# Another order of the same instructions in a fused adaLN block: V of the first pair loaded ahead of a LayerNorm group's transposes

## The chip, the cores and the metric

The kernel runs on one core of one Trainium2 chip. The metric is device time in microseconds, lower is better. Engines named below: PE (TensorE, matmuls and transposes), DVE (VectorE), ACT (ScalarE), POOL (GpSimd) and SP (SyncE, which here only issues DMAs). L851 is line 851 of the kernel.

## What is computed

One block on x of 2048 rows and 512 columns, in bf16, with six modulation vectors (sa, ca, ga, sb, cb, gb) made from one conditioning vector c:

```python
mod = (silu(c) @ w_mod).reshape(1, 6, 1, 512)          # sa, ca, ga, sb, cb, gb
h = layernorm(x) * (1 + ca) + sa
x = x + ga * A(h)      # 32 heads of 16, each row attends to itself and 7 rows before it, two apart
h = layernorm(x) * (1 + cb) + sb
x = x + gb * B(h)      # (silu(h @ w1) * (h @ w3)) @ w2, 1792 inner columns
```

In A, `qkv = h @ wqkv`; logits are `q . k / 4` over the 8 rows `s, s-2, ..., s-14` (rows before the first are masked), softmax over these 8, a weighted sum of v, and a product with `wo`.

## The kernel before

**Tiling.** The 2048 rows are 16 tiles of 128. Tile T holds the rows of one residue class modulo 16, so that a step of two rows is a step of one tile: tiles 0 to 7 are the even class, tiles 8 to 15 the odd one, and a tile's attention needs tiles of its own class only. SBUF holds all weights; `kT` holds k transposed for all rows.

**First stage, per group of tiles (`LN1`, L269: tiles 0-1, 2-3, 4-7, 8-11, 12-15).** `ln_stats` (L549) takes mean and variance on DVE (L555, L556), the power on POOL (L563, L565) and the normalised tile on DVE (L570). `ln_T` (L603) turns these into h: the first three groups by transposes on PE (L630) and a pass that applies the modulation on the way out of PSUM (DVE L645 or ACT L638); tiles 8-11 and 12-15 by four DMA transposes each (SP, L612 by the helper's L124) and four ACT passes (L615) that need all four. `proj_qk` (L669) makes q and k (PE L685, ACT copies L694 and L695), `proj_v` (L699) makes v (PE L705, ACT copy L715) and stores it to a scratch in DRAM. Four tiles share one q buffer: a product that reads it waits for the copies of all four.

**Attention, per pair of tiles (`BLOCKS`, L266).** `logits` (L727): DVE multiplies q with eight shifted k's (L742, L744), about 2.3 us a tile, and PE adds up within heads (L753). `shift`, `exps` and `softmax` (L760 to L814): maximum, difference, exponential on ACT (L783), sum, reciprocal and product on DVE, a turn on PE (L808) and a copy on ACT (L812). `values` (L816): two DMAs of 512 KB each load V of a tile from the scratch, already shifted (L823); they need the stores of all eight V tiles of the class and a free buffer of three. DVE multiplies with the weights (L829, called AV below, 2.29 us a tile), PE adds up (L839), ACT copies (L845), a DMA transposes (the tile `sb_ot`), PE multiplies with `wo`, scaled by ga before (L941, L851), and DVE adds to x with the row sum (L855).

**FFN, per group (`FFN`, L265: tiles 0-1, 2-3, 4-7, 8-11, 12-13, 14-15).** `ln_sums` (L576) on POOL and ACT (L580 to L595), `ln_T` again: by PE for the first two groups, by DMA transposes and ACT L615 for the others. `ffn_unit` (L860) makes one of 14 column groups: PE L867 for w1 and for w3, ACT silu (L873), DVE product (L876). `ffn_w2` (L883) multiplies with w2 (PE L908, at the end L896), and the result is scaled, added to x and stored.

**What sets the order.** `_build` lists 1121 operations, numbered as they are listed. `ORDER` (L975) is a permutation of these numbers written out by hand: `place` (L143) goes through it and appends each operation to its engine's queue, and `SLOTS` (L1024) gives each value its PSUM bank (0 to 7) or its buffer. Engines run their queues in this order; an operation waits for what it reads and for the last users of the bank or buffer that it takes over. So the order of each queue decides which wait stands in front of what. `GATES` (L974) adds dependencies to four weight loads. All DMAs but one are issued from SP's queue.

```python
for i in order: ...   # place: self.order[o.eng].append(o)
if before is not None:
    o.prev.extend(before.users)     # wait for the last users of this bank or buffer
```

Of the numbers that the next sections speak of: 368, 369 and 376, 377 are the V loads of tiles 0 and 1; 129, 135, 177, 183, 230, 233, 236, 239 the stores of V tiles 0 to 7; 256 to 259 the DMA transposes of tiles 8 to 11 and 308 to 311 those of tiles 12 to 15; 32 to 35 are loads of `wo`, 37 and 38 of a half each of a part of `w_mod`; 40 to 51 are FFN weights; 356, 358, 384, 386 the products of tiles 0, 1, 2 and 3; 370 and 378 the AVs of tiles 0 and 1; 763 to 766 the DMA transposes of FFN tiles 4 to 7; 513 and 521 the DMA transposes of the attention outputs of tiles 10 and 11; 480, 481, 488, 489, 508, 509, 516, 517 the V loads of tiles 8 to 11.

Of the kernel before, what the change touches and what calls it, by code (L numbers as in the profile page):

```python
# [271 lines left out]
def _build(p, A_x, A_wqkv, A_wo, B_w1, B_w3, B_w2, c, w_mod, out):  # L272
# [801 lines left out]
```

## Time and profile before

| what | value |
|---|---|
| median of 3 runs | 241.52 us (241.07 to 241.82) |
| the profiled execution's own time | 241.19 us |
| its span, first to last instruction | 239.4 us |
| PE busy | 231.6 us, 97% |
| DVE busy | 181.2 us, 76% |
| ACT busy | 142.5 us, 60% |
| POOL busy | 21.7 us, 9% |
| granted clock of PE | 1.00 |

The profile is of one execution. A row of a timeline gives the start, the time drawn, engine, line, operation, what it writes and reads, how many instructions are merged, and in brackets the idle time of the engine before it and what ended it. SPq is the issue of a DMA on SP; the landing is told apart from it (rows that begin with a time and DMA). The table by stage gives each engine's busy time within a stretch.

### The profile page before, as it was taken

What the parts mean: (1) busy time and instruction counts of PE and PEld (TensorE: products, weight loads), DVE (VectorE), ACT (ScalarE), POOL (GpSimd) and SP (SyncE); (2) the same over time, 40 slices, a digit from 0 to 9 for tenths busy, and PEclk for the clock granted to TensorE, in tenths of its full rate; (3) what the DMA queues carried; (4) which work ended last, traced back from release to release, by engine and by line L of the source; (5) the groups of instructions that cost most, each with busy time, mean ns of one, the idle gap of its engine ahead of it and who ended that gap; (6) DMA issues with size and microseconds to landing.
All of it is one profiled execution on the core that took longest, in us unless ns stands there. A gap on an engine that the chain in (4) does not pass through costs nothing.

```text
span 239.4 us, 4562 instructions
## 1 busy us (share of the span) xinstructions
PE 231.6 (97%) x1805; PEld 136.4 (57%) x1805; DVE 181.2 (76%) x309; ACT 142.5 (60%) x277; POOL 21.7 (9%) x63
## 2 busy tenths in 40 slices
PE   7999999899999999998998999999999999999995
PEld 4766454454678766553444445434448447576874
DVE  5689799897999999998969999746528365524562
ACT  2179978759999705975937786453665225451400
POOL 4134100001001000220003101000200002000000
PEclk9999999999999999999999999999999999999999
DMA  6999999969999898585370393613161100200012
GB/s 208 374 328 236 140 252 303 337 195 348 310 249 332 265 276 203 181 218 52 75 232 3 71 329 84 197 31 90 35 170 49 25 22 22 68 0 23 25 60 71
DMA packets 53997, 38.85 MB, mean 162 GB/s; under 512 B 21192, under 2 KB 52952, under 8 KB 53976
## 3 DMA queue, kind: packets, MB, share of 16 engines
q1 hardware_dynamic: 53968, 38.56, 58.1%
q8 instruction: 14, 0.23, 0.4%
q14 instruction: 7, 0.06, 0.1%
q10 hardware_dynamic: 8, 0.00, 0.0%
HBM read 29.62 MB, written 4.21 MB: 141 GB/s over the span
## 4 chain that ended last, share of the span: by engine, by line
PE 60%; DVE 14%; DMA 12%; ACT 6%; SPq 4%; issue 2%; POOL 1%; DVEq 0%
PE pall L867 34%; PE pall L908 14%; DMA sb_vsh<-v_scratch_dram 8%; DVE sb_vsh L829 5%; PE pall L851 4%; SPq L124 4%; DMA sb_wqkv<-in_A_wqkv_dram 3%; DVE sb_st L555 3%; PE pall L839 3%; PE pall L896 3%; DVE sb_pq L744 2%; DMA sb_h<-sb_xn 2%; DVE sb_xn L570 1%; ACT sb_h L615 1%; ACT sb_xn L595 1%
## 5 line engine op out<-in xcount | busy, mean ns | idle before, releaser
L867 PE MATMUL pall<-sb_h,sb_w 128*128 128x256 bf16 (+1 forms) x672 | 102.1, 308 | 1.2 <-ACT sb_h L615 1.2
L867 PEld LDWEIGHTS pall<-sb_h,sb_w 128*128 128x128 bf16 x672 | 64.8, 98 | 36.0 <-ACT sb_h L615 1.6
L876 DVE TENSOR_TENSOR sb_hh<-sb_sg,pall 128x256 bf16<-128x256 bf16 (+1 forms) x84 | 39.4, 504 | 30.8 <-PE pall L867 25.9
L873 ACT ACTIVATE sb_sg<-pall 128x256 bf16<-128x256 f32 (+1 forms) x84 | 35.0, 454 | 37.5 <-PE pall L867 32.4
L908 PE MATMUL pall<-sb_w,sb_hh 128*128 128x512 bf16 x168 | 37.7, 379 | 0.0
L685 PE MATMUL pall<-sb_h,sb_wqkv 128*128 128x512 bf16 (+1 forms) x160 | 31.8, 336 | 0.3 <-DMA sb_wqkv<-in_A_wqkv_dram 0.3
L829 DVE TENSOR_TENSOR sb_vsh<-sb_vsh,sb_al 128x4096 bf16<-128x4096 bf16 x12 | 27.2, 2290 | 5.6 <-DMA sb_vsh<-v_scratch_dram 5.6
L908 PEld LDWEIGHTS pall<-sb_w,sb_hh 128*128 128x128 bf16 x168 | 16.4, 98 | 18.7
L615 ACT ACTIVATE sb_h<-sb_h,sb_modc 128x512 bf16<-128x512 bf16 (+1 forms) x24 | 16.3, 733 | 12.1 <-DMA sb_h<-sb_xn 12.1
L685 PEld LDWEIGHTS pall<-sb_h,sb_wqkv 128*128 128x128 bf16 x160 | 14.9, 98 | 12.3 <-DVE sb_st L555 0.5
L742 DVE TENSOR_TENSOR sb_pq<-sb_q,sb_kT 128x1024 bf16<-128x1024 bf16 (+7 forms) x16 | 21.6, 1352 | 0.2 <-issue 0.2
L744 DVE TENSOR_TENSOR sb_pq<-sb_q,sb_kT 128x3048 bf16<-128x3048 bf16 (+6 forms) x14 | 17.2, 1226 | 0.0
L705 PE MATMUL pall<-sb_wqkv,sb_h 128*128 128x512 bf16 x64 | 16.8, 379 | 0.3 <-ACT sb_h L615 0.3
L584 ACT ACTIVATE sb_xn<-sb_x,sb_nm 128x512 bf16<-128x512 bf16 x16 | 11.4, 715 | 8.9 <-POOL sb_nm L580 8.9
L851 PE MATMUL pall<-sb_wo,sb_ot 128*128 128x512 bf16 x64 | 15.8, 380 | 0.3 <-DMA sb_ot<-sb_ac 0.3
L580 POOL TENSOR_SCALAR sb_nm<-sb_sx 128x2 f32<-128x2 f32 x8 | 1.7, 218 | 141.3 <-DVE sb_x L855 141.3
L595 ACT ACTIVATE sb_xn<-sb_x,sb_nb,sb_rs 128x512 bf16<-128x512 bf16 x16 | 12.6, 806 | 1.6 <-POOL sb_nb L593 1.6
L638 ACT ACTIVATE sb_h<-pall,sb_modc 128x256 bf16<-128x256 bf16 (+1 forms) x16 | 9.0, 625 | 7.0 <-DVE sb_modc L509 5.5
L855 DVE SCALAR_TENSOR_TENSOR sb_x<-pall,sb_x 128x512 bf16<-128x512 f32 x16 | 10.8, 686 | 1.3 <-PE pall L851 1.0
L694 ACT ACTIVATE sb_q<-pall 128x512 bf16<-128x512 f32 x16 | 9.2, 595 | 4.2 <-PE pall L685 4.2
L845 ACT ACTIVATE sb_ac<-pall 128x512 bf16<-128x512 f32 x16 | 9.4, 605 | 3.3 <-PE pall L839 3.3
L851 PEld LDWEIGHTS pall<-sb_wo,sb_ot 128*128 128x128 bf16 x64 | 6.0, 98 | 7.8 <-DMA sb_ot<-sb_ac 0.8
(88 smaller groups left out, 233.3 us busy)
## 6 DMA issues: line engine op xcount, KB each, us to landing
sb_vsh<-v_scratch_dram SPq DMA_DIRECT2D x24, 512.0 KB, 5.2
sb_vshx<-v_scratch_dram SPq DMA_DIRECT2D x8, 512.0 KB, 4.3
sb_w<-in_B_w_dram SPq DMA_DIRECT2D x6, 512.0 KB, 8.1
sb_w<-in_B_w_dram SPq DMA_DIRECT2D x6, 384.0 KB, 4.7
v_scratch_dram<-sb_v SPq DMA_DIRECT2D x16, 128.0 KB, 4.7
out_dram<-sb_o SPq DMA_DIRECT2D x14, 128.0 KB, 1.7
sb_wqkv<-in_A_wqkv_dram SPq DMA_DIRECT2D x6, 256.0 KB, 6.5
sb_x<-in_A_x_dram SPq DMA_DIRECT2D x4, 256.0 KB, 6.6
```

Of the source, the lines that this page charges most:

```text
L595: p.op("act", lambda e, vn=vn, T=T: e.activation(vn.at[:], x_sb[:, T, :], ACT.Identity, bias=nb[:, T, :], scale=rs[:, NT + T, :]), c_act(5 ...
L615: return e.activation(vh.at[:, ft, 0:n * P], vh.at[:, ft, 0:n * P], ACT.Identity, bias=modc[:, 8 * which + ft:8 * which + ft + 1], scale=m ...
L685: ins = e.matmul(bank(vp)[:, j * n:(j + 1) * n], wqkv[:, t, col:col + P], vh.at[:, t, 0:n], start=(t == ORDER[0] and j == 0), stop=(t == O ...
L705: ins = e.matmul(bank(vp), vh.at[:, t, tt * P:(tt + 1) * P], wqkv[:, t, 2 * D:3 * D], start=(t == ORDER[0]), stop=(t == ORDER[-1]))
L742: ins = e.tensor_tensor(o(0, u + 1, 0), q(u + 1, 0), k(T, u + 1, 0), ALU.mult)
L744: ins = e.tensor_tensor(o(u + 1, n, 1), q(n, 1), k(top, n, 1), ALU.mult)
L829: return e.tensor_tensor(v_w, v_w, a_w, ALU.mult)
L851: ins = e.matmul(bank(vy), vt.at[:, ft, :], wo[:, ft, :], start=(ft == 0), stop=(ft == KT - 1))
L867: ins = e.matmul(bank(vp)[:, 0:n], wt[:, t, fi * P:(fi + 1) * P], vh.at[:, t, 0:n], start=(t == 0), stop=(t == KT - 1))
L873: p.op("act", lambda e: e.activation(vt.at[:, 0:n], bank(vgp)[:, 0:n], ACT.Silu), c_act(n), k, r=[vgp], w=[vt], table="silu")
L876: p.op("dve", lambda e: e.tensor_tensor(vh_.at[:, 0:n], vt.at[:, 0:n], bank(vup)[:, 0:n], ALU.mult), c_dve(n), k, r=[vt, vup], w=[vh_])
L908: ins = e.matmul(bank(vz), vhh[fi].at[:, tt * P:(tt + 1) * P], scaled(fi, 0, D) if T >= NT - 4 else w2[:, fi, :], start=(fi == 0), stop=(f ...
```

## The change

`ORDER` and `SLOTS` are replaced; nothing else. Every operation is there once, as before. POOL's queue is the same. The other queues are the same up to the 16th DMA on SP, the 39th operation on PE, the 33rd on DVE and the 5th on ACT, and differ in most places behind that.

SP's queue behind the store of zeros (36), where the two begin to differ, by what each DMA moves:

| before | after |
|---|---|
| wo, wo, wo; V store 0, 3; w_mod gate (39); wo; V store 1 | w_mod half (37); V store 1, 0; wo, wo; w_mod gate (39) |
| transposes 8-11 (four); V store 5, 2 | transpose; V store 2; transpose; V store 6, 3; two transposes |
| two transposes of 12-15; w_mod half (37); V store 6, 4, 7 | V store 5, 4, 7; wo, wo; w_mod half (38) |
| FFN weight (45); two transposes of 12-15 | **V loads 0, 0, 1, 1** |
| **V loads 1, 1, 0**; V store 10; **V load 0** | FFN weights (40, 44); transposes of 12-15 (four) |
| FFN weight (42); w_mod half (38); V store 11, 13 | outputs' transposes of tiles 0, 1; V store 8, 9 |

Later on SP, around the DMA transposes of FFN tiles 4 to 7 (763 to 766) and of the outputs of tiles 10 and 11 (513, 521):

| before | after |
|---|---|
| 763; V loads 517 (tile 11), 481 (tile 8); 764, 765, 766 | V loads 509, 517, 516; 763, 764; V load 508 (tile 10); 765, 766 |
| 513; V load 489 (tile 9); 521; V loads 480, 488 | V load 489; 513; V load 488; 521; V loads 481, 542 (tile 12), 480 |

On DVE the products of tiles 0 and 1 come ahead of three normalised tiles (13, 14, 15) instead of one before and two behind; then follow the softmax, the products of tile 3, the AVs of tiles 0 and 1 and the products of tile 2 (before: products of 3, softmax, products of 2, AV 1, AV 0). On ACT the copy of q that the first products wait for (156) moves from the 18th place to the 27th, behind the copies of k. On PE v of tile 6 is the first of tiles 4 to 7 and v of tile 7 the eighth; `wo` of tiles 0 and 1 stands ahead of all q, k and v of tiles 12 to 15, which begin with q (318).

```diff
 ORDER = [
...
-    91, 92, 93, 94, 96, 100, 80, 95, 81, 82, 97, 101, 83, 98, 99, 84, 86, 85, 87, 119, 114, 104, 136, 138, 102, 109, 103, 36,
-    33, 32, 35, 110, 115, 120, 105, 137, 106, 121, 111, 116, 117, 112, 107, 108, 118, 113, 130, 139, 140, 141, 143, 145, 142,
-    144, 149, 148, 151, 150, 124, 125, 146, 131, 122, 123, 172, 126, 157, 147, 132, 152, 127, 128, 133, 129, 134, 173, 178,
-    179, 180, 158, 181, 167, 162, 163, 182, 183, 39, 34, 135, 184, 186, 185, 187, 194, 192, 195, 193, 188, 189, 191, 201, 207,
-    174, 168, 242, 190, 200, 196, 197, 206, 198, 208, 202, 199, 209, 211, 210, 203, 204, 205, 164, 175, 169, 170, 153, 154,
-    155, 344, 159, 156, 160, 165, 161, 166, 240, 241, 243, 248, 244, 250, 245, 247, 257, 345, 346, 249, 246, 251, 252, 256,
-    292, 294, 253, 255, 254, 259, 258, 295, 293, 296, 300, 297, 226, 227, 231, 232, 233, 171, 176, 177, 222, 223, 302, 301,
-    303, 304, 305, 307, 306, 310, 311, 220, 221, 224, 225, 358, 356, 299, 298, 37, 234, 235, 236, 347, 263, 261, 228, 229,
-    230, 237, 238, 212, 239, 260, 262, 218, 216, 219, 217, 359, 357, 386, 360, 361, 352, 214, 215, 348, 270, 271, 268, 269,
-    362, 363, 286, 287, 264, 276, 353, 354, 45, 309, 308, 314, 313, 277, 312, 364, 289, 365, 366, 367, 213, 377, 376, 369,
-    288, 368, 42, 278, 272, 315, 280, 279, 281, 290, 38, 291, 335, 336, 337, 322, 320, 384, 378, 323, 321, 379, 380, 370, 387,
...
-    755, 757, 764, 652, 503, 504, 717, 725, 756, 698, 718, 758, 505, 759, 730, 726, 760, 658, 731, 732, 761, 765, 506, 733,
-    507, 762, 766, 767, 768, 769, 770, 468, 734, 741, 735, 736, 737, 742, 743, 653, 510, 511, 469, 471, 518, 519, 520, 512,
-    472, 473, 524, 526, 771, 779, 775, 780, 659, 781, 782, 474, 475, 476, 477, 787, 789, 788, 790, 513, 514, 795, 515, 489,
-    521, 480, 803, 522, 523, 478, 479, 482, 488, 490, 799, 800, 823, 825, 791, 792, 824, 793, 796, 801, 525, 491, 527, 859,
...
+    91, 92, 93, 94, 96, 100, 80, 95, 81, 82, 97, 101, 83, 98, 99, 84, 86, 85, 87, 119, 114, 104, 136, 138, 102, 109, 103, 137,
+    110, 105, 115, 120, 121, 106, 116, 111, 122, 123, 124, 139, 140, 141, 143, 145, 142, 144, 146, 149, 148, 150, 147, 117,
+    107, 108, 118, 151, 130, 131, 178, 179, 172, 125, 173, 174, 162, 126, 36, 127, 37, 175, 128, 176, 132, 133, 134, 167, 168,
+    135, 129, 112, 157, 35, 34, 169, 39, 184, 186, 185, 187, 188, 189, 192, 194, 193, 195, 190, 206, 196, 200, 197, 170, 152,
+    191, 207, 201, 199, 203, 209, 198, 113, 171, 208, 211, 240, 241, 242, 243, 250, 248, 244, 245, 247, 257, 177, 202, 205,
+    210, 204, 251, 249, 292, 252, 253, 294, 255, 259, 300, 295, 293, 254, 296, 246, 153, 154, 155, 158, 163, 164, 297, 298,
+    180, 159, 160, 181, 165, 161, 344, 302, 234, 166, 235, 236, 182, 183, 256, 258, 224, 225, 345, 301, 226, 220, 303, 222,
+    304, 227, 305, 221, 223, 156, 358, 356, 231, 232, 233, 228, 229, 230, 237, 238, 239, 306, 307, 299, 261, 263, 262, 260,
+    346, 347, 216, 212, 359, 218, 357, 360, 361, 362, 219, 32, 33, 348, 352, 214, 215, 217, 283, 284, 280, 363, 274, 278, 281,
+    279, 275, 353, 364, 354, 365, 276, 366, 367, 266, 267, 264, 277, 270, 271, 265, 268, 269, 213, 38, 386, 387, 368, 369,
+    370, 371, 372, 377, 286, 376, 378, 379, 287, 380, 40, 44, 308, 311, 310, 309, 312, 315, 313, 355, 314, 349, 272, 273, 384,
...
+    705, 706, 733, 732, 734, 722, 709, 711, 689, 690, 757, 756, 758, 713, 712, 714, 759, 710, 506, 507, 760, 715, 716, 717,
+    761, 653, 765, 762, 766, 769, 768, 767, 770, 735, 718, 736, 737, 741, 742, 468, 518, 510, 471, 519, 469, 472, 473, 511,
+    512, 520, 526, 474, 475, 738, 739, 476, 477, 524, 819, 779, 787, 791, 788, 780, 820, 803, 775, 777, 478, 489, 513, 793,
+    514, 515, 776, 778, 792, 479, 488, 490, 521, 743, 804, 821, 805, 522, 523, 822, 806, 795, 799, 481, 542, 480, 482, 771,
...
 ]
 SLOTS = [
...
-    7, 0, 1, 2, 3, 4, 5, 6, 0, 1, 2, 3, 4, 5, 6, 0, 7, 1, 2, 3, 4, 5, 6, 0, 7, 3, 4, 5, 6, 0, 1, 1, 0, 2, 3, 0, 4, 7, 0, 2, 0,
-    1, 1, 3, 2, 5, 1, 6, 5, 7, 0, 6, 3, 2, 4, 2, 0, 4, 1, 2, 2, 2, 1, 3, 1, 1, 7, 5, 7, 5, 0, 4, 2, 0, 2, 0, 4, 1, 6, 2, 4, 3,
...
+    7, 0, 1, 2, 3, 4, 5, 6, 0, 1, 2, 3, 4, 5, 6, 0, 7, 1, 2, 3, 4, 5, 6, 0, 7, 3, 4, 5, 6, 0, 1, 1, 0, 2, 3, 0, 4, 7, 0, 1, 0,
+    2, 2, 3, 2, 5, 1, 6, 2, 6, 3, 7, 5, 1, 0, 0, 4, 0, 2, 1, 5, 2, 1, 4, 1, 0, 6, 2, 6, 3, 1, 5, 0, 2, 7, 1, 7, 2, 1, 0, 1, 3,
...
 ]
```

96 rows, old and new, of tables (ORDER, SLOTS) are left out of this document.

## The prediction

> **What bounds the kernel now.** I read the table of busy time by stage first, cut where the kind of work changes, then the timeline of PE for what ended each idle stretch, then DVE and the DMA issues (SPq) around each of them.
>
> ```profile
> 10.00:66.00 56.00, 54.94 (x497) 30.82 (x499) 49.96 (x82) 45.48 (x84) 7.72 (x18) 1.00 1.01 275
> 66.00:112.00 46.00, 46.00 (x444) 31.19 (x432) 44.61 (x75) 31.05 (x67) 4.17 (x12) 1.00 0.88 231
> 112.00:132.00 20.00, 17.93 (x130) 8.01 (x123) 17.62 (x20) 14.46 (x26) 2.59 (x4) 1.00 0.34 95
> 132.00:239.43 107.43, 104.81 (x679) 60.77 (x677) 62.62 (x113) 48.86 (x99) 4.51 (x13) 1.00 0.26 76
> ```
>
> The columns behind the length are PE, PE's weight loads, DVE, ACT and POOL, then clock, DMA share and GB/s. PE is idle 1.06 us from 10 to 66, nothing from 66 to 112, 2.07 from 112 to 132; the 2.62 behind 132 lie after its last matmul. The clock is 1.00 throughout. So PE sets the end, and an order of the same instructions can win only what PE waits.
>
> ```profile
> 41.80 1.04 PE L705 MATMUL pall<-sb_wqkv,sb_h 128*128 128x512 bf16 x4 [0.27 <-ACT sb_h L615]
> 46.65 0.61 PE L839 MATMUL pall<-sb_vsh,sb_ind 128*32 128x512 bf16 x8 [0.67 <-DVE sb_vsh L829]
> 113.44 0.82 PE L867 MATMUL pall<-sb_h,sb_w 128*128 128x512 bf16 x3 [1.15 <-ACT sb_h L615]
> 121.66 1.04 PE L851 MATMUL pall<-sb_wo,sb_ot 128*128 128x512 bf16 x4 [0.28 <-DMA sb_ot<-sb_ac]
> 122.76 5.34 PE L867 MATMUL pall<-sb_h,sb_w 128*128 128x512 bf16 x24
> 129.28 0.61 PE L839 MATMUL pall<-sb_vsh,sb_ind 128*32 128x512 bf16 x8 [0.63 <-DVE sb_vsh L829]
> ```
>
> A wait costs more than the idle shown. In the row of 24 matmuls, 5.34 us less one drawn length of 0.38 over 23 steps is 0.216 a matmul, so each drawn end lies 0.16 late. With 0.16 added: 0.43 and 0.83 in the opening, 1.31, 0.44 and 0.79 from 113 to 129: **3.8 us** in five waits, and some 0.3 in one small one at 61.6. That 4.1 is the most that can go.
>
> **The change.** Nothing is added or removed; POOL's order is the same. Everything up to 10 us is the same. Three places matter.
>
> **A, the opening (10 to 66).** The V loads of the first pair move on SP.
>
> ```profile
> 12.35 1.99 SPq L124 DMA_DIRECT2D sb_wo<-in_A_wo_dram  x3
> ...
> 30.42 1.49 SPq L124 DMA_DIRECT2D v_scratch_dram<-sb_v  x3
> ...
> 35.36 1.55 SPq L124 DMA_DIRECT2D sb_vsh<-v_scratch_dram  x3
> ...
> 37.51 0.66 SPq L124 DMA_DIRECT2D sb_vsh<-v_scratch_dram  x1
> ...
> 39.03 1.20 SPq L124 DMA_DIRECT2D sb_wm_s<-in_w_mod_dram  x1
> ```
> ```profile
> 25.53 0.73 DVE L570 TENSOR_SCALAR sb_xn<-sb_x,sb_mv,sb_rs 128x512 bf16<-128x512 bf16 x2 [1.08 <-POOL sb_rs L565]
> 26.47 0.68 DVE L742 TENSOR_TENSOR sb_pq<-sb_q,sb_kT 128x1024 bf16<-128x1024 bf16 x1 [0.20 <-issue]
> ...
> 38.35 0.95 DVE L742 TENSOR_TENSOR sb_pq<-sb_q,sb_kT 128x1536 bf16<-128x1536 bf16 x1
> 39.22 1.50 DVE L744 TENSOR_TENSOR sb_pq<-sb_q,sb_kT 128x2540 bf16<-128x2540 bf16 x1
> 41.09 2.29 DVE L829 TENSOR_TENSOR sb_vsh<-sb_vsh,sb_al 128x4096 bf16<-128x4096 bf16 x1 [0.37 <-DMA sb_vsh<-v_scratch_dram]
> 44.31 2.29 DVE L829 TENSOR_TENSOR sb_vsh<-sb_vsh,sb_al 128x4096 bf16<-128x4096 bf16 x1 [0.93 <-DMA sb_vsh<-v_scratch_dram]
> ```
> ```profile
> 24.67 1.74 ACT L695 ACTIVATE sb_kT<-pall 128x512 bf16<-128x512 f32 x3
> ```
>
> Now the four loads (two tiles, 512 KB each) start at 35.36 behind the store of V tile 7; two have landed when DVE starts at 41.09 (5.7 us) and all four at 44.31 (8.9 us). In the new list tile 7's matmuls are the eighth group of four (0.864 us) after PE takes up tiles 4 to 7, near 21.1 by the same work ahead of it: 21.1 + 7 x 0.864 + 1.0 = 28.2, ACT's copy takes 0.6 (below), and SP then issues this store (0.5), two parts of wo (0.66 each) and a w_mod half (1.2): the first load goes at about 32.1, three us sooner. Tile 0's V lands near 32.1 + 5.7 = 37.8, tile 1's near 41.0.
>
> DVE pays a little first. The first products now wait for the last of four q copies, which ACT takes behind all four k copies instead of ahead of them: one more ACT copy, start 26.75 for 26.47. From 26.47 to 40.72 DVE ran without a gap over 0.1; the new list has the same stretch with one normalisation more (0.33) and without tile 2's products (40.72 less 38.35, 2.28 of the queue's time): 14.25 - 1.95 = 12.3, so the AV of tile 0 starts at 39.05 and that of tile 1 at 41.3. Both V's are there, tile 1's by only 0.3. Behind them come tile 2's products, to 45.8, where DVE had done the same set at 46.6. The 0.37 and 0.93 go; 0.8 stays.
>
> PE loses some again: its row of tile 1's AV comes 0.5 ahead of DVE, tile 2's logits 0.2 ahead of the products, and wo of tile 1, next after tile 0's, some 0.3 ahead of its transposed input. The h of tiles 12 to 15 is the open cost. Its four transposes now stand behind four V loads and two FFN weights; I place their landing at 46.0 (bounds 44.2 and 50, worked out in the third rival), h after 2.93 us of ACT and one copy at 49.4, and PE's first need of it at 49.0: 0.4. Against 0.43 + 0.83 + 0.3 stand 0.5 + 0.2 + 0.3 + 0.2 (half of the last, since the three before it delay PE too). **A: -0.35**, bounds -1.55 and +4.
>
> From 66 to 112 PE has no idle now, and I find no bank or transfer in the new lists that comes later than PE's turn: 0, though DVE is busy 44.61 of 46.00, so a slip there reaches PE.
>
> **B, the h of the third FFN group (113.4).**
>
> ```profile
> 102.55 0.58 SPq L124 DMA_DIRECT2D sb_vshx<-v_scratch_dram  x1
> 103.17 0.51 SPq L124 DMA_DIRECT2D sb_vsh<-v_scratch_dram  x1
> 103.73 3.99 SPq L124 DMA_TRANSPOSE sb_h<-sb_xn  x3
> ```
> ```profile
> 106.45 3.97 DMA sb_h<-sb_xn
> 110.45 2.93 ACT sb_h L615 x4
> ```
> ```profile
> sb_h<-sb_xn SPq DMA_TRANSPOSE x20, 2.5
> ```
>
> Two V loads, 1 MB, are issued between the first and the second of four transposes; the last lands 3.97 us after its issue, against a median of 2.5 for all twenty, and ACT's four passes end where PE starts. In the new list one V load stands there, after the second transpose. On that row: 1.4 less in the landing, and the stretch ahead starts with A's 0.35. I place h at 110.6 to 111.8 and PE's arrival at 111.8 (now 112.14): **B: -1.3**, bounds 0 and -1.31.
>
> The Trainium skill, page "DMA: Bandwidth & Descriptors", section "Queues, rings and completion order", states that completion is not FIFO for one issuing engine: data descriptors carry no barrier, so a later one may finish first. By it the loads need not hold the transposes; the sum without B's 1.3 would then be 240.4. The row of 3.97 beside 2.5 speaks against it here, though one row does not prove the cause.
>
> **C, waits at 121.7 and 129.3.**
>
> ```profile
> 117.05 0.58 SPq L124 DMA_DIRECT2D sb_vsh<-v_scratch_dram  x1
> 117.68 1.19 SPq L124 DMA_TRANSPOSE sb_ot<-sb_ac  x1
> 118.91 1.19 SPq L124 DMA_DIRECT2D sb_vsh<-v_scratch_dram  x2
> ```
> ```profile
> 118.91 5.64 DMA sb_vsh<-v_scratch_dram
> 124.64 4.50 DVE sb_vsh L829 x2
> ```
>
> The first is wo of tile 11, whose transposed input stands behind a V load. PE's new list puts eleven groups of 0.864 and four small transposes (0.2), 9.7 us, between the FFN group's start and it, for 8.2 now (113.44 to 121.66): 1.5 covers 0.44, **-0.44** (0 to -0.44). The second is the AV of tiles 8 and 9, whose V is issued at 117 to 120 and lands 5.64 after issue. In the new list half of tile 9's V is issued ahead of the attention outputs' transposes, and tile 8's follows about 3 us sooner than now; DVE then needs two products (2.28 each), an AV (2.2) and eight shorter steps, 11.5 us in all, from the softmax that now starts at 111.9 to the end of AV 9; PE has 17 groups and two small steps, 15.3, before it wants that. I take **-0.6** of 0.79 (0 to -0.79), for AV 8 has half a us to spare.
>
> **D, behind 132.** PE never waits there now.
>
> ```profile
> 150.28 1.13 SPq L124 DMA_DIRECT2D sb_vsh<-v_scratch_dram  x2
> ...
> 155.75 2.29 DVE L829 TENSOR_TENSOR sb_vsh<-sb_vsh,sb_al 128x4096 bf16<-128x4096 bf16 x1 [1.65 <-DMA sb_vsh<-v_scratch_dram]
> ```
>
> The V of tile 15 takes 5.5 us from first issue to use, and DVE waits 1.65. In the new list its buffer is freed by PE's row of tile 13, and a product behind AV 15 frees the bank of PE's row of tile 14. Chain: 0.6 + 5.5 + 2.3 + 0.9 and steps, 9.4 to 10.4; PE has seven FFN groups, two of wo, half an output (1.5) and two AV rows (0.44 each), 10.2, between. **D: +0.25** (0 to 0.6).
>
> **Sum.** -0.35 - 1.3 - 0.44 - 0.6 + 0.25 = -2.44 against the profiled execution's 241.19: 238.75. The median of the three runs, 241.52, lies 0.33 above that execution, so I forecast **239.1**, own range 237.9 to 240.5.
>
> **Rivals.**
> - Every wait goes and no new one comes: 241.5 - 4.1 = 237.4. For it: the waits are all DMA landings, which the list can move. Against: 0.3 us to spare in A.
> - The transposes take 3.97 by themselves, as under the page's rule: 240.4. Or the waits form again at the same size with DVE at 97% in the middle stage: 241.5.
> - **Slower: the transposes of tiles 12 to 15 starve PE.** From 30.9 SP queues 0.52 MB of w_mod, 2.10 of V, 0.91 of FFN weights ahead of them, 3.5 MB.
>
> ```profile
> GB/s 208 374 328 236 140 252 303 337 195 348 310 249 332 265 276 203 181 218 52 75 232 3 71 329 84 197 31 90 35 170 49 25 22 22 68 0 23 25 60 71
> ```
>
> The seventh and eighth slices (36 to 48) ran at 303 and 337: 3.53 / 0.32 = 11 us, then 2.5 for a transpose and 0.5 for each of the next three, 46; 44.2 if the last three come with the first and at 337. At the ninth slice's 195 it is 18 us: 50 or more. From 45.6 each us of lateness is a us of PE, for its next ten 512-column groups all want this h. The outputs' transposes queue behind as well. Slower than 241.5 by over 0.7 takes a landing at 49.1; at 50, 243.0.
>
> **Chances.** Forecast 0.49; all waits gone 0.12; transposes' own time 0.08; waits re-formed 0.07; starved 0.24. A measurement of this kernel tells some 0.3% (0.72 us) from no change. Faster: 0.49 + 0.12 + 0.06 = 0.67; same 0.02 + 0.05 + 0.01 = 0.08; slower 0.02 + 0.23 = 0.25. The range leaves out the better half of the second case (0.06) and just over half of the starved one (0.13): 237.3 to 242.9.
>
> **What would show it.** A: the two L829 of the first pair have no DMA releaser, and PE's idle from 10 to 66 stays near 1; if PE waits over 1 us for ACT L615 between 45 and 52, the starved case holds. B: PE's idle before its first 512-column L867 is under 0.7. C: no idle before L851 near 120 and before L839 near 127. D: one idle under 0.6 near 162. Wrong would be: idle in the middle stage, or any PE wait over 1 us that is not named here.

## The result, and the profile after

The changed kernel takes 241.00 us (median of 12, 240.59 to 241.51) beside 241.68 us for the kernel before (12 runs beside them); the ratio is **0.9952, 95% interval 0.9932 to 0.9972**. A second set of 12 gave 0.9961 (0.9931 to 0.9992). So it is faster, by about 0.4 to 0.5%, or 1 us; forecast were 2.4. Both sets lie above the forecast's range, which ended at 240.5. The profiled execution took 241.46 us, among the longer ones of its 12, with a span of 239.6; the profile of the second set has 240.93 and 239.1.

First the table by stage (columns as before: length, PE, weight loads, DVE, ACT, POOL, clock, DMA share, GB/s).

```profile
10.00:66.00 56.00, 53.19 (x462) 28.96 (x468) 48.12 (x80) 44.47 (x81) 7.76 (x18) 0.97 0.97 258
66.00:112.00 46.00, 45.55 (x405) 31.42 (x409) 44.88 (x75) 33.10 (x70) 3.94 (x12) 1.00 0.86 240
112.00:132.00 20.00, 19.63 (x172) 9.46 (x174) 19.62 (x22) 14.11 (x24) 0.22 (x1) 1.00 0.48 143
```

PE's idle time has changed places: 2.81 us in the opening for 1.06, 0.45 from 66 to 112 for nothing, and 0.37 from 112 to 132 for 2.07. No wait shows behind the 0.45: this profile has 1778 matmul records for 1805 weight loads (the kernel before has 1805 of both), and where a record is missing a gap is drawn, most of them of 0.05 and none over 0.16. The opening also has a clock of 0.97. PE's timeline names the waits.

```profile
45.31 0.61 PE L839 MATMUL pall<-sb_vsh,sb_ind 128*32 128x512 bf16 x8 [1.59 <-DVE sb_vsh L829]
49.77 2.05 PE L851 MATMUL pall<-sb_wo,sb_ot 128*128 128x512 bf16 x7 [0.67 <-DMA sb_ot<-sb_ac]
...
115.01 5.99 PE L867 MATMUL pall<-sb_h,sb_w 128*128 128x512 bf16 x27 [0.16 <-ACT sb_o L919]
121.93 1.03 PE L851 MATMUL pall<-sb_wo,sb_ot 128*128 128x512 bf16 x4
...
124.52 1.03 PE L851 MATMUL pall<-sb_wo,sb_ot 128*128 128x512 bf16 x3
...
130.24 0.60 PE L839 MATMUL pall<-sb_vsh,sb_ind 128*32 128x512 bf16 x8
...
167.81 8.58 PE L867 MATMUL pall<-sb_h,sb_w 128*128 128x512 bf16 x39 [0.16 <-issue]
```

The waits of B and C (113, 121 and 129 before; now the rows at 115.01, 124.52 and 130.24) are gone. The gaps of 0.16 are missing records: the first weights of the row at 115.01 are loaded at 114.78, so it begins at 114.8. For the third FFN group the chain that ended last shows the landing of B's last transpose and ACT's passes:

```profile
108.89 2.53 DMA sb_h<-sb_xn
111.44 2.93 ACT sb_h L615 x4
```

The transpose lands in 2.53 us (3.97 before). The h is ready at 114.37, not at 110.6 to 111.8, since all of this stretch comes later, and it is ready 0.4 us ahead of PE.

In the opening PE stands 1.59 us in front of the row of AV 1 and 0.67 in front of wo of tile 0. Here too the first matmul's record is missing: its weights are loaded at 49.37, so some 0.4 of the 0.67 is no wait. Why PE waits is shown by DVE, SP and ACT.

```profile
34.46 1.23 DVE L941 TENSOR_TENSOR sb_wo<-sb_wo,sb_ga_bc 128x2048 bf16<-128x2048 bf16 x1 [0.74 <-DMA sb_wo<-in_A_wo_dram]
39.79 2.28 DVE L829 TENSOR_TENSOR sb_vsh<-sb_vsh,sb_al 128x4096 bf16<-128x4096 bf16 x1
42.96 2.29 DVE L829 TENSOR_TENSOR sb_vsh<-sb_vsh,sb_al 128x4096 bf16<-128x4096 bf16 x1 [0.89 <-DMA sb_vsh<-v_scratch_dram]
```
```profile
30.23 1.24 SPq L124 DMA_DIRECT2D sb_wo<-in_A_wo_dram  x2
31.51 0.59 SPq L124 DMA_DIRECT2D sb_wm_s<-in_w_mod_dram  x1
32.29 2.74 SPq L124 DMA_DIRECT2D sb_vsh<-v_scratch_dram  x4
35.07 2.83 SPq L124 DMA_DIRECT2D sb_w<-in_B_w_dram  x2
37.94 8.83 SPq L124 DMA_TRANSPOSE sb_h<-sb_xn  x4
46.81 2.58 SPq L124 DMA_TRANSPOSE sb_ot<-sb_ac  x2
```
```profile
48.92 2.22 ACT L615 ACTIVATE sb_h<-sb_h,sb_modc 128x512 bf16<-128x512 bf16 x3 [2.35 <-DMA sb_h<-sb_xn]
```

The first V load goes out at 32.29, as forecast (32.1), but V of tile 1 is there only at 42.9 (10.6 us later, not 8.9), and the transposes of tiles 12 to 15 only at 48.9 (not 46.0). The reason shows at the two parts of wo, issued from 30.23 to 31.47: the second lands at 34.4 and holds DVE until 34.46. What SP issues behind them lands in its turn: the w_mod half of 31.51 at 36.3, V of tile 0 at 39.2, V of tile 1 at 42.9, the last FFN weight at 45.4, the last transpose at 48.9.

Last, the clock around these waits.

```profile
44.00:47.00 3.00, 1.69 (x42) 1.13 (x43) 3.00 (x3) 0.94 (x2) 0.00 (x0) 1.00 1.36 78
47.00:50.50 3.50, 2.83 (x22) 1.00 (x21) 2.80 (x3) 1.58 (x3) 0.00 (x0) 0.52 0.75 149
50.50:54.00 3.50, 3.50 (x17) 1.56 (x16) 2.76 (x7) 3.40 (x7) 0.22 (x1) 1.00 0.83 240
```

Behind the wait at 45 PE is granted half its clock for 3.4 us. Most of that falls into the time up to 49.37, when it would have waited for the transposed output anyway (it lands at 49.33). The eight matmuls of wo behind it take 2.29 us, to 51.66, for 1.73 at 0.216 each: 0.6 us. In the second set's execution (waits of 1.14 and 1.44 us) the clock stays at 1.00.

### The profile page after: what moved, and what is told of

The parts are those of the page before. It is cut to its first block, busy times and chain, and to the rows that moved or that the text cites. A ratio compares the mean times of both kernels' runs of the same rounds, so it can differ in the third digit from the quotient of the medians.

```text
span 239.6 us, 4529 instructions
## 1 busy us (share of the span) xinstructions
PE 230.6 (96%) x1778; PEld 136.3 (57%) x1805; DVE 181.7 (76%) x309; ACT 143.6 (60%) x277; POOL 21.6 (9%) x63
## 4 chain that ended last, share of the span: by engine, by line
PE 49%; ACT 2%; DMA 2%; DVE 1%; issue 0%; SPq 0%
PE pall L867 30%; PE pall L908 12%; PE pall L896 3%; PE pall L851 3%; DMA sb_h<-sb_xn 2%; ACT sb_h L615 1%; PE pall L839 1%; DVE sb_x L855 1%; PE pall L753 0%; PE pall L808 0%; DVE sb_o L920 0%; ACT sb_sg L873 0%; ACT sb_al L812 0%; ACT sb_o L919 0%; DVE sb_o L926 0%
## 5 line engine op out<-in xcount | busy, mean ns | idle before, releaser
L867 PE MATMUL pall<-sb_h,sb_w 128*128 128x256 bf16 (+1 forms) x667 | 100.9, 308 | 0.8 <-issue 0.3
L867 PEld LDWEIGHTS pall<-sb_h,sb_w 128*128 128x128 bf16 x672 | 64.8, 98 | 35.6 <-issue 1.2
L685 PE MATMUL pall<-sb_h,sb_wqkv 128*128 128x512 bf16 (+1 forms) x158 | 31.3, 339 | 0.3
L829 DVE TENSOR_TENSOR sb_vsh<-sb_vsh,sb_al 128x4096 bf16<-128x4096 bf16 x12 | 27.3, 2285 | 3.2 <-DMA sb_vsh<-v_scratch_dram 3.2
L615 ACT ACTIVATE sb_h<-sb_h,sb_modc 128x512 bf16<-128x512 bf16 (+1 forms) x24 | 16.2, 732 | 10.4 <-DMA sb_h<-sb_xn 10.3
L851 PE MATMUL pall<-sb_wo,sb_ot 128*128 128x512 bf16 x58 | 15.3, 386 | 1.0 <-DMA sb_ot<-sb_ac 0.7
L705 PE MATMUL pall<-sb_wqkv,sb_h 128*128 128x512 bf16 x58 | 14.7, 379 | 0.3 <-issue 0.2
L695 ACT ACTIVATE sb_kT<-pall 128x512 bf16<-128x512 f32 x16 | 9.4, 595 | 3.0 <-PE pall L685 2.9
L919 ACT ACTIVATE sb_o<-pall 128x512 bf16<-128x512 f32 x12 | 7.1, 601 | 5.8 <-PE pall L908 5.8
```

Source lines behind the costliest of these rows:

```text
L615: return e.activation(vh.at[:, ft, 0:n * P], vh.at[:, ft, 0:n * P], ACT.Identity, bias=modc[:, 8 * which + ft:8 * which + ft + 1], scale=m ...
L685: ins = e.matmul(bank(vp)[:, j * n:(j + 1) * n], wqkv[:, t, col:col + P], vh.at[:, t, 0:n], start=(t == ORDER[0] and j == 0), stop=(t == O ...
L705: ins = e.matmul(bank(vp), vh.at[:, t, tt * P:(tt + 1) * P], wqkv[:, t, 2 * D:3 * D], start=(t == ORDER[0]), stop=(t == ORDER[-1]))
L829: return e.tensor_tensor(v_w, v_w, a_w, ALU.mult)
L851: ins = e.matmul(bank(vy), vt.at[:, ft, :], wo[:, ft, :], start=(ft == 0), stop=(ft == KT - 1))
L867: ins = e.matmul(bank(vp)[:, 0:n], wt[:, t, fi * P:(fi + 1) * P], vh.at[:, t, 0:n], start=(t == 0), stop=(t == KT - 1))
```

## The experiments

Ratios are to the kernel before, run on the same chip; in brackets the 95% interval. The times behind them are medians. They come from four chips (the yardstick, e1, e2, e3, e10, e11; e4 to e7; e8, e9; e12), on which the kernel before takes 242.26 to 242.61 us, so a difference between kernels of two chips holds to some 0.4 us. A diff shows SP's queue by the operations' numbers, as far as it changes; unless a diff says otherwise, the other queues and the buffers stay as they are.

**The yardstick.** 

> The changed kernel once more, as the yardstick of the next three on the same chip. By every theory about 241.0 us, 0.2 to 0.7% below the kernel before, with PE's two waits in the opening again: about 1.6 us in front of the row of AV 1 (L839) near 45 and about 0.7 in front of wo of tile 0 (L851) near 50. If the half clock (granted 0.50 near 49) came from the particular execution, it may be missing here; if it follows from PE's idle time alone, it is there again.

0.9961 (0.9931 to 0.9992), median 241.22. Waits of 1.14 in front of AV 1's row and 1.44 in front of wo of tile 0, as said above. The half clock belongs to some executions only: 4 of these 12 runs, and 2 of the first 12, have a mean granted clock of 0.993 or less (3.4 us at half take 0.007 off the mean), the others 0.999 or 1.00. These 4 took 241.35 to 242.99 us, the other eight 240.46 to 241.35.

**One thing out of the way of each.**

```diff
-38, 368, 369, 377, 376, 40, 44, 308, 311, 310, 309, 373, 381, 282, 285, 405, 46, 404, 396, 397, 291, 288, 42, 45, 47
+38, 368, 369, 377, 376, 308, 311, 310, 309, 373, 381, 282, 285, 405, 46, 404, 396, 397, 291, 288, 42, 44, 40, 45, 47
```

> The changed kernel, with the two FFN weight loads (40, 44) moved on SP from between the V loads of the first pair and the transposes of h of tiles 12 to 15 to behind FFN weight 42. Theory queue (what stands ahead on SP's queue sets when a transfer lands): the last of the four transposes lands at 46.4 for 48.9, the transposed output of tile 0 near 47 for 49.3, PE's wait in front of wo of tile 0 (0.7) goes, the wait for AV 1 (1.6) stays as the V loads are not touched: 0.8 to 1.3 us less than the changed kernel, 239.7 to 240.2. Rival order (PE's new order asks too early, wherever the loads stand): another wait takes its place, within 0.3 us of the changed kernel. Rival transposes' own time: their issue keeps its 8.8 us for four and the landing stays near 48.9; no gain.

0.9924 (0.9896 to 0.9952), 240.58: 0.6 under the yardstick by the medians, with intervals that overlap. The wait for wo is gone, the one for AV 1 is there, and a small one for an FFN weight is new:

```profile
44.77 0.62 PE L839 MATMUL pall<-sb_vsh,sb_ind 128*32 128x512 bf16 x8 [1.02 <-DVE sb_vsh L829]
47.87 1.69 PE L851 MATMUL pall<-sb_wo,sb_ot 128*128 128x512 bf16 x7 [0.16 <-issue]
65.51 1.05 PE L867 MATMUL pall<-sb_h,sb_w 128*128 128x256 bf16 x8 [0.38 <-DMA sb_w<-in_B_w_dram]
```

```diff
-32, 33, 38, 368, 369, 377, 376, 40
+32, 33, 368, 369, 377, 376, 38, 40
```

> The changed kernel, with the half of w_mod (38) moved on SP from ahead of the four V loads of the first pair to right behind them. Theory queue: V of tile 1 lands 1.8 sooner (41.1 for 42.9), DVE has no wait for it, the row of AV 1 starts at 44.3 for 45.3; but the transposes and the outputs' transposes behind them land as before, so PE waits the rest in front of wo of tile 0 (about 1.6 for 0.7): within 0.4 us of the changed kernel. Rival V alone: the late V of tile 1 is the whole loss, and the kernel gains 1.0 us, 240.0.

0.9986 (0.9958 to 1.0014), 242.36: no gain, and 1.1 over the yardstick, though the intervals overlap and the profiled execution was 0.6 us late already when the first V load went out (32.84 for 32.29). About half of the 1.1 is the clock: 7 of the 12 runs have a mean of 0.993 or less (242.29 to 243.64), and the median of the other five, 241.54, is 0.6 over that of the yardstick's eight. The wait moved as expected, from AV 1 to wo:

```profile
45.13 0.62 PE L839 MATMUL pall<-sb_vsh,sb_ind 128*32 128x512 bf16 x8 [0.62 <-DVE sb_vsh L829]
50.18 0.81 PE L851 MATMUL pall<-sb_wo,sb_ot 128*128 128x512 bf16 x3 [2.11 <-DMA sb_ot<-sb_ac]
```

> Both moves together. Theory queue: the two waits overlap in the changed kernel and go only together; PE reaches q of tiles 12 to 15 near 50.1 for 52.5, so 2.0 to 2.4 us less than the changed kernel, 238.6 to 239.0, if nothing behind 66 takes it back. Rival middle stage (DVE, busy 97% there, takes back what PE wins in the opening): the opening is shorter by 2, but PE waits for DVE between 66 and 112 and the gain is under 1 us. Rival order: no more than the sum of the two single moves.

0.9902 (0.9867 to 0.9937), 239.86: 1.4 under the yardstick, more than the two moves apart (-0.6, +1.1), less than the 2.0 to 2.4 expected. None of its seven runs has a clock under 0.999. The waits for AV 1 and the transposed output are gone; wo of tile 0 starts at 47.22 for 49.21 in the yardstick. But a part comes back as waits for FFN weights:

```profile
47.22 1.70 PE L851 MATMUL pall<-sb_wo,sb_ot 128*128 128x512 bf16 x7 [0.16 <-issue]
61.82 0.61 PE L867 MATMUL pall<-sb_h,sb_w 128*128 128x256 bf16 x4 [0.26 <-DMA sb_w<-in_B_w_dram]
64.61 0.60 PE L867 MATMUL pall<-sb_h,sb_w 128*128 128x256 bf16 x4 [0.45 <-DMA sb_w<-in_B_w_dram]
65.54 1.05 PE L867 MATMUL pall<-sb_h,sb_w 128*128 128x256 bf16 x8 [0.32 <-DMA sb_w<-in_B_w_dram]
```
```profile
44.00:50.00 6.00, 5.81 (x74) 2.86 (x75) 6.00 (x10) 4.97 (x8) 0.07 (x1) 1.00 0.48 107
50.00:64.00 14.00, 13.63 (x118) 7.14 (x117) 12.93 (x13) 13.32 (x27) 1.25 (x4) 1.00 1.10 351
```

By the table of e3, DMA moves 107 GB/s from 44 to 50, as SP stands in front of the outputs' transposes, and 351 from 50 to 64. The busy share of its engines is 0.48 and 1.10: in e3 DMA has room up to 50 and none behind.

**Filling that hole: three tries.** On e3, weight 42 goes into the hole, ahead of the outputs' transposes (e7, with two stores moved as well; e8 without) or right behind them (e11).

```diff
 e7: 308, 311, 310, 309, 42, 373, 381, 405, 46, 404, 396, 397, 282, 285, 291, 288, 44, 40, 45, 47
 e8: 308, 311, 310, 309, 42, 373, 381, 282, 285, 405, 46, 404, 396, 397, 291, 288, 44, 40, 45, 47
 e11: 308, 311, 310, 309, 373, 381, 42, 282, 285, 405, 46, 404, 396, 397, 291, 288, 44, 40, 45, 47
```

> The kernel with both moves (e3), and FFN weight 42 moved on SP to right behind the transposes of h of tiles 12 to 15, where DMA moved 115 GB/s from 44 to 50 while SP waited to issue the outputs' transposes; the stores of V of tiles 8 and 9 go behind the V loads of tiles 2 and 3. Theory lull (in e3 PE waits 1.0 us for FFN weights between 61 and 66, as DMA is full from 50 to 64): the weights land 1.5 to 2.5 us sooner, these waits go, 1.0 to 1.5 us less than e3, 238.4 to 238.9, ratio to the kernel before 0.984 to 0.986. Rival outputs: weight 42 holds the outputs' transposes, and PE waits over 0.7 us in front of wo of tile 0 again: e3's time or more. Rival middle stage: the waits go, and PE waits for DVE behind 66: e3's time within 0.3.

1.0129 (1.0076 to 1.0183), 245.89. The wait that the rival outputs named is there (0.73 in front of wo at 47.54), but the loss is another, which none of the expectations had. ACT's copy of a V tile waited 4.12 us for the buffer that the moved store (282) was to empty, and PE 3.86 us behind it; the clock fell too (0.50 from 56.7 to 63.5, in this profile).

```profile
56.65 0.60 ACT L715 ACTIVATE sb_v<-pall 128x512 bf16<-128x512 f32 x1 [4.12 <-DMA v_scratch_dram<-sb_v]
```

> The previous kernel (e7) with the stores of V of tiles 8 and 9 (282, 285) put back ahead of the V loads of tiles 2 and 3; FFN weight 42 stays right behind the transposes of h of tiles 12 to 15, and 38, 40, 44 stay behind as in e3. Theory store (in e7 ACT's copy of v of tile 11 waited until 57.2 for the moved store of tile 8 to land at 56.6, held ACT's queue behind it, and PE stood 3.86 us and ran at half clock for 3.4 more): all of e7's loss goes, and the weights land 1.0 to 1.5 us sooner than in e3: 0.8 to 1.3 us less than e3, ratio to the kernel before 0.985 to 0.988. Rival weight (weight 42 in the lull is what cost e7 its time): slower than the kernel before, as e7. Rival no gain: e3's ratio, 0.990, with PE's waits for weights near 62 to 66 as in e3.

0.9916 (0.9884 to 0.9949), 240.37: the stores were e7's loss, and the weight brings nothing over e3. It held the outputs' transposes, PE waiting 1.51 us for wo of tile 0 (48.88).

> The kernel with both moves (e3) and FFN weight 42 right behind the outputs' transposes of the first pair (381) instead of ahead of them (as e8) or eleven issues later (as e3). Theory restart (each time SP stands in front of an issue, the queue runs empty, and the next load lands some 4 us behind its issue: 42 then fills what stands empty between 47.8 and 51.7): 42 lands near 50.5, the V loads of tiles 2 and 3 within 0.5 us of e3, the weights 44, 40, 45, 47 1.0 to 1.3 us sooner, no wait over 0.3 us in front of wo of tile 0, and PE's 1.0 us for weights between 61 and 66 goes: 0.8 to 1.2 us less than e3, ratio to the kernel before 0.985 to 0.987. Rival bytes (the queue's rate, not its holes, sets when all has landed): what 42 gains the V loads of tiles 2 and 3 lose, AV 3 and AV 2 come late by 1.2 and PE waits there: e3's time.

0.9913 (0.9883 to 0.9943), 240.47: e3's time within the intervals, so the rival holds. What weight 42 gained, the V loads of tiles 2 and 3 lost; PE waits 0.44 and 1.31 us for AV 3 and AV 2 (60.59, 63.40).

**The named part undone, and alone.** In e5 the changed kernel has the transposes ahead of the V loads again; in e6 the kernel before has the last two of them behind.

```diff
 e5
-38, 368, 369, 377, 376, 40, 44, 308, 311, 310, 309, 373
+38, 308, 311, 310, 309, 368, 369, 377, 376, 40, 44, 373
 e6
-239, 45, 309, 308, 377, 376, 369, 288, 368, 42, 38
+239, 45, 377, 376, 369, 288, 368, 309, 308, 42, 38
```

> The changed kernel with its named part undone: on SP the four transposes of h of tiles 12 to 15 stand ahead of the four V loads of the first pair, all else as changed. Theory queue: the transposes land near 39.5 for 48.9, V of tiles 0 and 1 at 42.7 and 45.7 for 39.2 and 42.9, PE waits some 3 us in front of the row of AV 0, and as its row of AV 1 and wo of tile 0 come later too: 1.0 to 1.8 us more than the changed kernel, 242.2 to 243.0. Rival: the late transposes are the whole loss of the opening; then this order gains 0.8 or more on the changed kernel, 240.4 or less.

1.0098 (1.0062 to 1.0134), 244.77: 3.5 over the yardstick (3.3 by the ratios), twice what was expected.

> The kernel before with the named part alone: on SP the last two transposes of h of tiles 12 to 15 (309, 308) moved behind the V loads of the first pair, all else as before. Theory queue: V of the pair lands 1 us sooner and DVE's waits (0.37 and 0.93) go, but the two transposes land near 45.6 for 37.3 and PE, whose old list asks for this h at 41.6, waits until 48: 4 to 5 us more, ratio 1.017 to 1.021. Rival: PE finds the time again behind it, as the rows of AV 0 and 1 no longer wait: under 2 us more.

1.0333 (1.0246 to 1.0420), 251.15: 8.6 over the kernel before (242.56), also twice. The directions hold: with the changed orders V first is worth 3.5 us, with the old orders it costs 8.6. What both sizes lacked is mostly the clock. In e5 the waits are 1.4 us more than the yardstick's (3.47 and 0.52 for 1.14 and 1.44), as expected, but every one of its 11 runs lost clock, and the times follow it: 243.70 to 244.32 us at a mean of 0.993, 244.77 to 245.64 at 0.986, 246.14 to 246.24 at 0.979. First a PE row of e5, then PE rows and the table of e6:

```profile
45.79 0.63 PE L839 MATMUL pall<-sb_vsh,sb_ind 128*32 128x512 bf16 x8 [3.47 <-DVE sb_vsh L829]
```
```profile
37.73 1.03 PE L705 MATMUL pall<-sb_wqkv,sb_h 128*128 128x512 bf16 x4
...
47.64 1.89 PE L705 MATMUL pall<-sb_wqkv,sb_h 128*128 128x512 bf16 x4 [6.93 <-ACT sb_kT L695]
```
```profile
36.00:47.00 11.00, 4.71 (x28) 2.16 (x26) 4.74 (x7) 2.14 (x4) 0.00 (x0) 0.83 0.98 294
47.00:53.00 6.00, 4.88 (x12) 1.51 (x13) 4.20 (x2) 5.01 (x10) 0.00 (x0) 0.50 0.25 77
```

Behind e6's wait of 6.93 the same four matmuls take 1.89 us for 1.03, and PE runs at 0.50 until 53.6, for 6 us: a loss of nearly 3 us, as its matmuls take about twice as long. Another us is ACT: it stands at L615 until the transposes land (45.56), so the copy L695 behind it comes late too, and PE, whose wait this copy ends, stops at 40.6, not at 41.6. A long wait is paid once while it lasts and here again behind it.

**The gain behind 112, alone.**

```diff
-763, 517, 481, 764, 765, 766, 513
+763, 517, 764, 765, 766, 481, 513
```

> The kernel before, with one of the two V loads (481) that stand between the DMA transposes of the third FFN group moved behind the last of them (766); nothing else. Theory queue: the last transpose lands 1.4 us sooner (109.0 for 110.4), PE's 1.15 us idle in front of its first 512-column L867 goes: 1.2 to 1.4 us less than the kernel before, ratio 0.994 to 0.995. Rival transposes' own time (a V load in front does not hold them): landing, wait and time as before, ratio 1.000. Rival DVE: the wait moves to the AV of tiles 8 and 9, whose V (481) is now later: ratio 0.998 to 1.000 with a longer wait in front of the row of AV 9 near 129.

0.9958 (0.9927 to 0.9988), 241.33: 1.2 under the kernel before (242.56). Its chain of waits has the landing at 2.70 us (3.97 before), and L867 starts without idle time:

```profile
108.18 2.70 DMA sb_h<-sb_xn
110.90 2.93 ACT sb_h L615 x4
```

In this execution PE came to L867 1.9 us later than before (114.00 for 112.14), after longer waits in the opening; e9, below, shows the same landing and no wait with PE on time. But a wait of 1.56 us, behind ACT and POOL, is new at 136.28 in this execution, one of the longer of its 12 (242.57). It comes back in e10, below.

**DMA moves alone in the kernel before.** The orders of PE, DVE, ACT and POOL are those of before.

```diff
-311, 37, 236, 230, 239, 45, 309, 308, 377, 376, 369, 288, 368, 42, 38, 291, ..., 763, 517, 481, 764, 765, 766
+311, 236, 230, 239, 309, 308, 377, 376, 369, 288, 368, 37, 42, 38, 45, 291, ..., 763, 517, 764, 765, 766, 481
```

> The kernel before with DMA issues moved on SP alone, every other queue as before: a half of w_mod (37) and FFN weight 45 from ahead of the four V loads of the first pair to behind them, and the V load 481 behind the transposes of the third FFN group (766). Theory queue: V of the pair lands 2.5 us sooner, the waits for AV 1 and AV 0 (0.37 and 0.93 on DVE, 0.83 on PE) and for h of tiles 12 to 15 (0.43) go, and the 1.31 at 113: 2.3 to 2.7 us less than the kernel before, 0.989 to 0.9905. Rival order (the gain of the changed kernel behind 66 needs its new orders of PE, DVE and ACT): not more than the 0.4% of the one load alone (e4). Rival later: the weight 45 and the half 37 are then late for PE or DVE near 52 to 67, half of the gain.

0.9903 (0.9868 to 0.9937), 240.14: 2.2 under the kernel before (242.32), by the medians twice the gain of the change; the intervals just overlap. DVE's product with V of tile 0 starts at 43.26 for 44.31, PE's wait for it is 0.19, the third FFN group starts at 111.88 for 113.44, without a wait:

```profile
43.26 2.29 DVE L829 TENSOR_TENSOR sb_vsh<-sb_vsh,sb_al 128x4096 bf16<-128x4096 bf16 x1 [0.47 <-DMA sb_vsh<-v_scratch_dram]
```
```profile
111.88 5.36 PE L867 MATMUL pall<-sb_h,sb_w 128*128 128x512 bf16 x24
```

A wait of 0.73 in front of wo of tile 1 is new (50.51).

```diff
 on e9
-42, 38, 45, 291, ..., 397, 282, 343, 44, ..., 766, 481, 513, 489, 521, 480, 488
+42, 38, 291, ..., 397, 282, 343, 45, 44, ..., 766, 481, 480, 513, 489, 521, 488
```

> The kernel of e9 (the kernel before with DMA moves on SP alone) with two moves more: FFN weight 45 from ahead of the outputs' transposes of the first pair to behind the stores of V of tiles 8 and 15 (282, 343), and the second V load of tile 8 (480) from behind the outputs' transposes of tiles 10 and 11 to right behind 481. Theory queue: the transposed output of tile 1 lands 1.4 us sooner and PE's 0.73 in front of wo of tile 1 goes; V of tile 8 is there 9 us sooner, AV 8 starts as soon as DVE is free, and the 0.26 in front of the row of AV 9 goes: 0.8 to 1.3 us less than e9, 238.9 to 239.4, ratio to the kernel before 0.985 to 0.987. Rival later: weight 45 is then late for PE near 66, or DVE, not the V load, sets AV 9: ratio as e9, 0.990.

0.9939 (0.9915 to 0.9963), 240.83: 0.7 more than e9 (on another chip; the intervals overlap), so no gain. The waits for wo of tile 1 and AV 9 went as expected. In the opening V of tile 0 landed late in this execution (0.90 in front of its row, 0.19 in e9), and a wait of 1.55 appeared behind 132. Rows of PE, ACT, POOL and DVE:

```profile
134.43 1.06 PE L753 MATMUL pall<-sb_pq,sb_E 128*32 128x256 bf16 x32 [1.55 <-ACT sb_sg L873]
```
```profile
133.08 0.81 ACT L595 ACTIVATE sb_xn<-sb_x,sb_nb,sb_rs 128x512 bf16<-128x512 bf16 x1 [3.00 <-POOL sb_nb L593]
```
```profile
127.96 1.95 POOL L590 TENSOR_SCALAR sb_rs<-sb_var 128x2 f32<-128x2 f32 x1 [5.72 <-ACT sb_xn L584]
129.99 0.76 POOL L591 TENSOR_TENSOR sb_rs<-sb_rs,sb_cst 128x2 f32<-128x2 f32 x1
130.84 2.21 POOL L593 TENSOR_TENSOR sb_nb<-sb_nm,sb_rs 128x2 f32<-128x2 f32 x1
```
```profile
127.84 2.02 DVE L742 TENSOR_TENSOR sb_pq<-sb_q,sb_kT 128x3584 bf16<-128x3584 bf16 x1
...
130.71 2.28 DVE L742 TENSOR_TENSOR sb_pq<-sb_q,sb_kT 128x4096 bf16<-128x4096 bf16 x1
```

POOL's L590, 0.19 us elsewhere in this profile, begins 0.12 behind DVE's product and ends 0.05 behind its end (129.86); L593 does the same under the next product (which ends at 132.99). In e4 L590 took the same 1.95, again begun 0.12 behind the product (129.81 and 129.69); in e9 it took 0.19 and began 0.42 ahead of it (127.68 and 128.10). So half a us of start time decides.

```diff
 DVE, on e10
-794, 528, 532, 530
+794, 532, 528, 530
```

> The kernel of e10 with one swap on DVE: the reduction of the softmax of tiles 12 and 13 (532, L765) ahead of the products of tile 14 (528, L742) instead of behind them. In e10 the product began at 127.84 and POOL's L590 at 127.96, ended with the product at 129.9, and L593 ended with the next product at 133.04 for ACT and PE to wait for. Theory product (a product of DVE holds a POOL instruction that begins under it until its end): L590 takes 0.2 us again and ends near 128.2, L593 is done at 130.9 or sooner, ACT's L595 starts 2 us sooner and PE's 1.55 in front of the logits of tile 14 near 134.4 goes: 1.2 to 1.6 us less than e10, 239.2 to 239.6, ratio to the kernel before 0.987 to 0.989. Rival own time: L590 and L593 take 1.9 and 2.2 us wherever they stand, the wait stays over 1 us, ratio 0.994 as e10. Rival swap: the products of tiles 14 and 15 come later by 0.6 and PE waits for them instead: 0.991 to 0.993.

**0.9877 (0.9840 to 0.9914), 239.54**, the lowest ratio of the study, though its interval overlaps those of e3 and e9: 1.3 under e10, as expected. L590 is short again, and L593 done 2.6 us sooner; it still runs under the product, which now begins at 128.36, and takes 1.73 us for 0.20, but PE does not wait for it:

```profile
127.65 0.19 POOL L590 TENSOR_SCALAR sb_rs<-sb_var 128x2 f32<-128x2 f32 x1 [5.72 <-ACT sb_xn L584]
127.92 0.71 POOL L591 TENSOR_TENSOR sb_rs<-sb_rs,sb_cst 128x2 f32<-128x2 f32 x1
128.71 1.73 POOL L593 TENSOR_TENSOR sb_nb<-sb_nm,sb_rs 128x2 f32<-128x2 f32 x1
```

PE's wait behind 132 is gone.

## Why the forecast missed

The direction was right, the size was not: of the 2.4 us forecast came 0.7 by the medians of the first set and 1.3 by those of the second. Terms against the profiled executions:

| term | forecast | measured | from |
|---|---|---|---|
| A and middle | -0.35 | +2.7 (second set +2.1) | PE at the third FFN group at 114.8 (114.3) without a wait, for 113.44 - 1.31 = 112.13; the same 241 operations stand ahead of it in both lists |
| B | -1.3 | -1.31 | the wait at 113.4 is gone |
| C | -0.44, -0.6 | -0.44, -0.79 | both waits are gone |
| D | +0.25 | 0 | no idle over 0.16 near 162 |

The sum is +0.1 (second set -0.4); the executions differ by 241.46 - 241.19 = +0.27 (240.93: -0.26), so some 0.15 is not accounted for. That the medians show more of a gain, 0.7, lies in before's profiled execution, which was 0.5 under the median of the 12 runs.

**The step that failed** is in A, the only term that came out wrong by more than 0.25: "Tile 0's V lands near 32.1 + 5.7 = 37.8, tile 1's near 41.0", and with it "I place their landing at 46.0". I carried over a time from issue to landing that in the kernel before started with little ahead of it in the queue, and I counted the rate of 0.32 MB per us from the issue at 30.9. The rate was right, the start was not: wo, issued just ahead, landed at 34.4, and the 0.5 MB of w_mod was still to come. From 34.4 the 3.53 MB take 11 us at that rate, 45.4, where the last FFN weight does land, and the transposes are there at 48.9. V of tile 0 landed at 39.2 and V of tile 1 at 42.9, for 37.8 and 41.0. The price list beside it was too short as well: DVE waited 0.74 for wo (its AV 0 started at 39.79 for the 39.05 forecast), and the outputs' transposes, of which the third rival says only that they queue behind, were the last to land and set PE's second wait. e1 takes 0.9 MB from ahead of the transposes and gains 0.6; e2 takes 0.5 MB from ahead of V alone and gains nothing, as the second wait then takes what the first gives back; e3 takes both, loses both waits and gains 1.4. So these two waits are the queue's, laid one over the other.

They are not all of A. In the second set, where the clock stayed at 1.00, they cost 1.3 and 1.4 us, and a wait for the h of tiles 12 to 15 0.2 (PE takes it up at 52.00, for 51.80); before's waits of 1.56 there are gone, as forecast. That leaves about 0.8 of the 2.1 to PE's new list itself, for which the prediction had no term. PE loses some 0.4 near 12, where it now asks for normalised tiles (L570) ahead of their time (e2 and e3 show it as a wait of 0.35). And it changes to the small matmuls of L753 and L839 and back 11 times ahead of the third FFN group, for 8 before. A change costs about 0.2 us by the changed kernel's rows, 0.6 for three: eight L839 take 0.44 us from 62.36 to the next such row and 0.55 from 63.67 to L867, and PE comes to such rows some 0.1 late (30.02, for 29.93 at 0.216 a matmul). These two are read from the rows; no run tests them.

**The rivals.** The starved case had the landing right and the wait wrong. The transposes landed at 48.9, near the 49.1 that it named as decisive, but its sign, a wait of PE of over 1 us for ACT L615, did not come: the h was ready at 52.32, 0.2 ahead of PE, which had been held by V of tile 1 and by the transposed output. (Its lower bound of 44.2 comes to 43.9 by its own figures.) The forecast's own signs failed in A (the second L829 still waits 0.89 for its V, and PE waits 1.59 where 0.5 was named) and held in B and C; of the idle named for D there was none. B and C were won in full, so the kernel ended faster and not at 241.5. The h of B was ready only 0.4 us ahead of PE (0.3 in the second set and in e3), so it came later as PE did. The transposes' own time is refuted for these transfers: with one 512 KB load less ahead of them (e4) the last took 2.70 for 3.97, and as long in e9. On that rule of the Trainium skill (page "DMA: Bandwidth & Descriptors", section "Queues, rings and completion order"): loads and transposes may finish out of order by it, yet here every landing of the 136 DMAs on SP's queue came in the order of issue, in each of these traces.

**What the change is worth.** The named part is not a gain by itself (e6, +8.6 us); it needs PE's order to ask for this h later, and then it is worth 3.5 (e5). But the new orders of PE, DVE and ACT were not needed for the gain: three DMAs moved in the old lists (e9) give at least as much, twice as much by the medians. Not tried was whether e12's moves and the change's orders add up.

## What to carry to other kernels

Price a moved DMA by all that the queue still has to move when it is issued, not by the time that the same load took elsewhere, and count what queues behind it. Where several waits in a row have the same queue as their cause, taking away one shows nothing: list them all with their landings, and move the transfer that nobody needs yet. A wait that goes makes engines start sooner, and what they then run into (a buffer not yet stored, a short instruction under a long product) can cost as much as the wait did.

## What the runs showed of the hardware

**The clock behind a wait.** PE ran at half clock for 3.4 us behind a wait of 1.59 us in the changed kernel's profile, but not behind waits of 1.14 and 1.44 (second set), 1.51 (e8) or 2.11 us (e2); in e6, with its wait of 6.93 us, it did for 10.2, from 43.3 on, inside the wait. The runs without a profile tell more: a mean granted clock of 0.993 or less is in 2 and 4 of 12 runs of the changed kernel, 3 of 12 of e1, 7 of 12 of e2, in every run of e5, e6 and e7 (longest waits 3.47, 6.93 and 3.86 us), and in none of the other experiments. So behind waits of one to two us it came in some executions and not in others, and behind waits of over 3 us it came each time here. The Trainium skill (page "TensorE: Matmul & The Clock Gate", section "Part 1: The HAM clock gate") says that PE's activity is watched in free-running windows of some 3.4 us and that an idle window halves the clock. The traces agree with the length; that a wait of 1.59 us was enough, though PE was busy for 1.69 us of the 3.00 from 44 to 47, is not explained by it.

**POOL under DVE's products.** An instruction of 0.19 us took 1.95 when it began 0.12 us behind a product of DVE (e4, e10), and 0.19 again with a reduction in the product's place (e12). The Trainium skill (page "SBUF — State Buffer", section "Who interferes with whom") states that a DVE instruction with two SBUF inputs contends with a GpSimd instruction that reads SBUF, and that contention at the port pair which the two share is "an exclusive lock". e10 and e12 agree; the price here was 1.55 us of PE, three engines away from DVE.
